# A chunked delta-rule attention with two dense layers: the first block solve done as two 16-row triangles joined by products, and the weights loaded from ScalarE's queue

## The chip, the cores and the metric

The kernel runs on one core of one Trainium2 chip. The metric is the device time of one execution in microseconds (us); the times below are those of three executions and of one profiled execution. The engines are TensorE (PE, matrix products), VectorE (DVE), ScalarE (ACT), GpSimd (POOL) and SyncE (SP, which only issues transfers).

## What is computed

A linear attention with a delta rule for each of 4 x 8 heads over 768 steps, with a state of 48 x 48 for each head; its output (3072 tokens of 384) runs through two dense layers.

```python
k_n = k / (np.linalg.norm(k, axis=-1, keepdims=True) + 1e-06)
for t in range(S):
    kt, vt, bt = (k_n[:, :, t], v[:, :, t], beta[:, :, t, None])
    y[:, :, t] = np.einsum('bhd,bhde->bhe', q[:, :, t], state)
    v_old = np.einsum('bhde,bhd->bhe', state, kt)
    state = state + bt[:, :, :, None] * np.einsum('bhd,bhe->bhde', kt, vt - v_old)
...
h = x @ w_in                       # 384 -> 1024
solu = h * softmax(h)
ln = (solu - mu) / np.sqrt(var + 1e-06) * g_ln
x = ln @ w_out                     # 1024 -> 384
...
h = x @ w_in                       # 384 -> 2048
g = h * (1.0 / (1.0 + np.exp(-1.702 * h)))
y = g @ w_out                      # 2048 -> 384
```

## The kernel before, in words

The 768 steps are cut into 24 chunks of 32 (`CH`), numbered n; four chunks are a macro step m. Within a chunk the rule is solved for all steps at once: with the products of the chunk's normalised k vectors in a lower triangle, the inverse of that triangle, applied to v minus what the state already holds, gives the chunk's updates. The parts are functions, and each of them adds tasks to a planner.

- `weights` (lines 443 to 506), called 42 times by `all_weights`: one slice of a weight matrix. The matrices come as 8-byte floats. SP issues the load of the raw words (L462, the only place where weights are loaded), ACT takes the high word's magnitude (L465), DVE merges the low word's bits and the sign in three steps (L467, L469, L477), ACT makes the fp16 high part (L490), PE forms the rest by products with an identity (L496, L497) and ACT stores it as the fp16 low part (L499), or DVE does it alone (L502). Staging buffers are few (`stg`, and pieces of other tensors lent to it while those are unused), so a load's issue waits until the slice before in its buffer is done. Every dense product later is three fp16 products of high and low parts.
- `gram(n)` (lines 545 to 581): PE forms k by k and k by q for the chunk (L554), DVE masks them (L569), SP stores both to DRAM (L579, L581), which turns them round for the solve.
- `solve(m)` (lines 584 to 660), one system of 32 x 32 for each of 128 rows (4 chunks x 8 heads x 4 batches) side by side on DVE: the load of the triangles `tri` (L588), norms by three steps of an iteration (L596 to L610), a scaling of `tri` (L615), ones on the diagonal (L618) and the elimination. Step j multiplies column j of the rows below j by row j (L624) and adds it to those rows (L627). For m = 0 this is one task, `whole`, with each step cut in two pieces; for m > 0 the 60 instructions are 60 tasks among DVE's other work. Then the inverse is scaled into `dsb` (L643), stored (L653) and loaded back by chunk as `dt` (L658).
- `recur(n)` (lines 661 to 798), the chain through the state: v is scaled on POOL (L714); for n > 0 PE applies the state to k (L726) and DVE subtracts (L730), giving `r_`; PE multiplies `r_` by the chunk's inverse (`dr_`, L735, 32 small fp32 products); ACT copies the result beside the state (L742; from a certain n on DVE does half of them, L746); PE forms the chunk's output (L752) and the state's update (L787, or L782), which DVE adds (L796).
- `layer1(n)` (lines 801 to 887): DVE takes the output's scale (L816), it is split into fp16 parts and transposed, PE multiplies by `w1` (L834), then softmax and normalisation on DVE, ACT and POOL (L841 to L881), and a transpose into `lnt` (L887). `layer1_out(g)` works on a group of 2 or 4 chunks: products with `wo1` (L906), written as `x2th` by ACT (L910) and `x2tl` by DVE (L913). `layer2(g)`: `w2` (L941), the gate (L946 to L958), `wo2` (L968), and the store of the result.

`busy` (L344, L345) lets PE multiply zeros wherever the planner sees it idle in the early part; below these are the filler products.

The order is a planner's (`Plan`): it is a list scheduler with a cost for every task, run while the program is built. A task's priority is the due time of its chunk (`due`) plus constants from `PRM` and an offset from the table `OFF`. It writes one fixed stream per engine, and on the chip each engine runs its stream strictly in order, waiting at semaphores. So everything in an engine's stream behind a waiting instruction waits too. A DMA task's issue stands in the stream of the engine that issues it. The order in which the functions are called, in the loop at the end of the kernel, gives the dependencies: before the change, `gram(4..7)` and `solve(1)` are called ahead of `recur(0)`.

```python
for n in range(first[g], first[g] + cnt):
    if n % SUB == 0 and n // SUB + 1 < NMAC:
        for n2 in range(n + SUB, n + 2 * SUB):
            gram(n2)
        solve(n // SUB + 1)
    layer1(n, recur(n))
layer1_out(g)
layer2(g)
```

## Time and profile before

| | us |
|---|---|
| median of 3 executions | 838.25 |
| lowest, highest | 837.28, 838.33 |
| profiled execution, time | 838.51 |
| profiled execution, span of the profile | 836.8 |

The profiled execution's time is 1.7 us more than its span: that lies outside the instructions that the profile records. All times of the trace count from the span's start. A line L462 is line 462 of the kernel before. "A<-B" beside a time means that the engine waited for A's producer B.

### The profile page before, as it was taken

What the parts mean: (1) busy time and instruction counts of PE and PEld (TensorE: products, weight loads), DVE (VectorE), ACT (ScalarE), POOL (GpSimd) and SP (SyncE); (2) the same over time, 40 slices, a digit from 0 to 9 for tenths busy, and PEclk for the clock granted to TensorE, in tenths of its full rate; (3) what the DMA queues carried; (4) which work ended last, traced back from release to release, by engine and by line L of the source; (5) the groups of instructions that cost most, each with busy time, mean ns of one, the idle gap of its engine ahead of it and who ended that gap; (6) DMA issues with size and microseconds to landing.
All of it is one profiled execution on the core that took longest, in us unless ns stands there. A gap on an engine that the chain in (4) does not pass through costs nothing.

```text
span 836.8 us, 25071 instructions
## 1 busy us (share of the span) xinstructions
PE 765.9 (92%) x10461; PEld 415.1 (50%) x10461; DVE 595.7 (71%) x1557; ACT 375.8 (45%) x695; POOL 252.0 (30%) x249
## 2 busy tenths in 40 slices
PE   6538889999899999998999999999999999999997
PEld 3224555677666744444444444444545444444443
DVE  1896978999998978999889889996655456311111
ACT  1425734466555513455543455345553436422332
POOL 3002010232214433434531445324442314330322
PEclk7658999999999999999999999999999999999999
DMA  7797878966666465638874365346543333011001
GB/s 177 226 254 178 225 158 192 241 105 173 151 123 168 99 137 149 156 90 187 161 203 125 91 167 107 102 127 153 136 64 92 114 60 47 16 26 38 1 0 38
DMA packets 177745, 105.75 MB, mean 126 GB/s; under 512 B 128320, under 2 KB 161984, under 8 KB 177632
## 3 DMA queue, kind: packets, MB, share of 16 engines
q1 hardware_dynamic: 177632, 104.15, 53.0%
q8 instruction: 82, 1.34, 0.7%
q14 instruction: 31, 0.25, 0.1%
HBM read 66.16 MB, written 20.64 MB: 104 GB/s over the span
## 4 chain that ended last, share of the span: by engine, by line
PE 35%; DVE 14%; issue 3%; ACT 2%; DMA 1%; SPq 1%; POOL 0%; POOLq 0%; ACTq 0%; DVEq 0%
PE psum L941 11%; PE psum L968 11%; PE psum L906 5%; PE psum L834 4%; DVE trt L624 2%; DVE tri L627 2%; DVE th L949 1%; DVE mv L746 1%; DVE mv L796 1%; PE psum L735 1%; PE psum L752 1%; ACT mv L742 1%; DMA stg<-udr 1%; PE psum L726 1%; DVE eb L853 1%
## 5 line engine op out<-in xcount | busy, mean ns | idle before, releaser
L955 POOL TENSOR_TENSOR gl<-th,gh 128x512 f16<-128x512 f32 (+1 forms) x105 | 114.2, 1089 | 226.4 <-ACT gh L952 154.3
L949 DVE SCALAR_TENSOR_TENSOR th<-th,psum 128x512 f32<-128x512 f32 (+1 forms) x112 | 67.8, 607 | 85.8 <-ACT th L946 85.2
L968 PE MATMUL psum<-gh,wo2h 128*128 128x512 f16 (+1 forms) x336 | 117.8, 350 | 1.6 <-ACT ob L979 1.2
L968 PE MATMUL psum<-gl,wo2h 128*128 128x512 f16 (+1 forms) x336 | 117.5, 350 | 1.7 <-POOL gl L955 1.4
L968 PE MATMUL psum<-gh,wo2l 128*128 128x512 f16 (+1 forms) x336 | 117.4, 350 | 1.1 <-ACT wo2l L499 1.1
L941 PE MATMUL psum<-x2th,w2h 128*128 128x512 f16 (+1 forms) x336 | 117.8, 351 | 0.3 <-DVE ysb L823 0.2
L941 PE MATMUL psum<-x2th,w2l 128*128 128x512 f16 (+1 forms) x336 | 117.6, 350 | 0.0
L941 PE MATMUL psum<-x2tl,w2h 128*128 128x512 f16 (+1 forms) x336 | 117.6, 350 | 0.0
L946 ACT ACTIVATE th<-psum 128x512 f32<-128x512 f32 (+1 forms) x112 | 59.3, 531 | 97.4 <-PE psum L941 96.9
L952 ACT ACTIVATE gh<-th 128x512 f16<-128x512 f32 (+1 forms) x112 | 63.2, 566 | 74.5 <-DVE th L949 72.7
L968 PEld LDWEIGHTS <-wo2h 128*128 128x128 f16 x672 | 65.8, 98 | 62.3 <-issue 4.5
L834 PE MATMUL psum<-w1h,xt 128*128 128x512 f16 x288 | 93.6, 384 | 2.3 <-DMA xt<-ysb 1.4
L941 PEld LDWEIGHTS <-w2h 128*128 128x128 f16 x672 | 64.2, 98 | 57.2 <-issue 0.6
L624 DVE TENSOR_TENSOR trt<-tri 128x58 f32<-128x58 f32 (+29 forms) x209 | 80.3, 395 | 2.8
L627 DVE TENSOR_TENSOR tri<-tri,trt 128x58 f32<-128x58 f32 (+29 forms) x209 | 79.0, 390 | 2.3
L834 PEld LDWEIGHTS <-xt 128*128 128x128 f16 x432 | 41.3, 99 | 51.0 <-issue 3.9
L850 ACT ACTIVATE eb<-psum,col 128x512 f32<-128x512 f32 x48 | 36.9, 772 | 61.2 <-DVE col L846 53.2
L796 DVE SCALAR_TENSOR_TENSOR mv<-psum,mv 48x384 f32<-48x384 f32 x92 | 51.0, 555 | 16.5 <-PE psum L782 14.1
L883 POOL TENSOR_TENSOR lnr<-eb,lnr 128x1024 f16<-128x1024 f32 x24 | 51.3, 2139 | 35.7 <-ACT lnr L881 35.7
L906 PE MATMUL psum<-lntl,wo1h 128*128 128x512 f16 (+1 forms) x168 | 58.6, 349 | 0.9 <-DMA lntl<-lnr 0.9
L906 PE MATMUL psum<-lnth,wo1h 128*128 128x512 f16 (+1 forms) x168 | 58.6, 349 | 0.0
L906 PE MATMUL psum<-lnth,wo1l 128*128 128x512 f16 (+1 forms) x168 | 58.6, 349 | 0.0
(191 smaller groups left out, 1228.3 us busy)
## 6 DMA issues: line engine op xcount, KB each, us to landing
kq<-kq SPq DMA_DIRECT2D x44, 192.0 KB, 4.6
stg<-w_in SPq DMA_DIRECT2D x11, 512.0 KB, 5.9
vt<-vt SPq DMA_DIRECT2D x24, 192.0 KB, 3.5
st<-qt SPq DMA_DIRECT2D x48, 96.0 KB, 2.4
stg<-udr SPq DMA_DIRECT2D x48, 96.0 KB, 2.4
kt<-kdr SPq DMA_DIRECT2D x48, 96.0 KB, 2.8
ktr<-kd SPq DMA_DIRECT2D x46, 96.0 KB, 3.5
stg<-w_out SPq DMA_DIRECT2D x11, 384.0 KB, 5.5
```

The lines of the kernel that those rows point to most:

```text
L624: DVE.tensor_tensor(out=tv, in0=tri[:, lo:hi, j:j + 1].to_broadcast([128, nr, j]), in1=tri[:, j:j + 1, 0:j].to_broadcast([128, nr, j]), op ...
L627: DVE.tensor_tensor(out=tri[:, lo:hi, 0:j], in0=tri[:, lo:hi, 0:j], in1=tv, op=ALU.add)
L796: P.add("DVE", dve(384), lambda sv=sv, r0=r0, e=e: DVE.scalar_tensor_tensor(out=sv, in0=bank(b4[e])[r0:r0 + D, 0:H * D], scalar=1.0 / (KS_ ...
L834: PE.matmul(bank(bh[j]), lhsT=x[:, k], rhs=w_[:, k, 512 * j:512 * j + 512], start=(k == 0 and i == 0), stop=(k == K0 - 1 and i == 2))
L883: P.add("POOL", pool(F1), lambda: POOL.tensor_tensor(out=lnr[1], in0=e_, in1=lnr[0], op=ALU.subtract), r=["lnrh"] + [f"eb{ie}_{j}" for j i ...
L906: PE.matmul(bank(ba)[:, 0:w_], lhsT=wo1[a][:, k, oc], rhs=lnt[b][:, k, tk], start=(k == 0 and i == 0), stop=(k == K1 - 1 and i == 2))
L941: PE.matmul(bank(bh)[:, 0:w_], lhsT=w2[a][:, k, fc], rhs=x2t[b][:, k, tk], start=(k == 0 and j == 0), stop=(k == K0 - 1 and j == 2))
L946: P.add("ACT", act(w_), lambda: ACT.activation(out=th, in_=bank(bh)[:, 0:w_], func=ACTF.Tanh, scale=0.851 / (X2S * W2S)), r=[bh], w=[f"th{ ...
L949: P.add("DVE", dve(w_), lambda: DVE.scalar_tensor_tensor(out=th, in0=th, scalar=1.0, in1=bank(bh)[:, 0:w_], op0=ALU.add, op1=ALU.mult), r= ...
L952: P.add("ACT", act(w_), lambda: ACT.activation(out=gh, in_=th, func=ACTF.Copy), r=[f"th{i}"], w=[f"gh{i}"], prio=base)
L955: P.add("POOL", pool(w_), lambda: POOL.tensor_tensor(out=gl, in0=th, in1=gh, op=ALU.subtract), r=[f"th{i}", f"gh{i}"], w=[f"gl{i}"], prio= ...
L968: PE.matmul(bank(acc[o])[:, 0:w_], lhsT=wo2[a][:, f, oc], rhs=gb[i][b][:, 0:w_], start=(f == 0 and j == 0), stop=(f == K2 - 1 and j == 2))
```

## The change

The first system (m = 0) is no longer eliminated whole. `halves` sets the lower left 16 x 16 block to zero and eliminates the two 16 x 16 triangles on the diagonal at once, by a view `blocks` of the tensor that has the two triangles as a second axis. The inverse that it leaves is block diagonal. What is missing, the effect of the first 16 steps of a chunk on the last 16, is put into the recurrences of chunks 0 to 3: `first_` applies the block-diagonal inverse to `r_`, ACT copies the result, `over_` multiplies it by the lower left block of the k products (`below`, which `gram` now keeps for these chunks, masked by `cross`), DVE subtracts that from `r_`, and then `dr_` runs as before. Weight loads are issued by ACT instead of SP, somewhat earlier in priority, and the planner keeps a DMA clock for each of the two issuers. `gram(4..7)` and `solve(1)` are called behind `recur(3)`. One tile of zeros serves both uses. All numbers in `OFF` and `PRM` are new.

```diff
+    trip = T("trip", [128, CH * CH + CH])
+    tri = trip[:, 0:CH * CH].rearrange("p (i j) -> p i j", j=CH)
+    blocks = trip.rearrange("p (a x) -> p a x", a=2)[:, :, 0:512].rearrange("p a (i c) -> p a i c", c=CH)
+    cross = T("cross", [128, CH])
...
+        def corner():
+            POOL.memset(cross, 1.0)
+            POOL.memset(cross[:, 0:CH // 2], 0.0)
+            for b in range(B):
+                x = cross[32 * b:32 * b + 32, CH // 2:]
+                POOL.affine_select(out=x, in_=x, pattern=[[0, CH // 2]], base=CH // 2,
+                                   channel_multiplier=-1, compare_op=ALU.is_gt, fill=0.0)
...
-            P.add("SP", ISSUE, lambda: SP.dma_start(out=raw.rearrange("p n t -> p (n t)"), in_=src.bitcast(I32)),
-                  w=key, prio=prio, lat=dma(n * 1024), nb=PRM["nb"] if nst[0] <= PRM["nk"] else PRM["nb2"])
+            P.add("ACT", ISSUE, lambda: ACT.dma_start(out=raw.rearrange("p n t -> p (n t)"), in_=src.bitcast(I32)),
+                  w=key, prio=prio - PRM["wl"], lat=dma(n * 1024), nb=PRM["nb"] if nst[0] <= PRM["nk"] else PRM["nb2"])
...
         if m == 0:
+            P.add("DVE", dve(256), lambda: DVE.tensor_tensor(
+                out=below[s], in0=bank(bk).rearrange("p (h c) -> p h c", h=H)[:, :, 0:CH],
+                in1=cross.unsqueeze(1).to_broadcast([128, H, CH]), op=ALU.mult),
+                r=[bk, "cross"], w=[belowk[s], f"below{s}"], prio=base + PRM["bl"])
...
-            def whole():
-                for j in range(1, CH - 1):
-                    mid = j + 1 + max(1, round((CH - 1 - j) * PRM["cut"]))
-                    cuts = [(j + 1, mid), (mid, CH)] if mid < CH else [(j + 1, CH)]
-                    for part in range(2):
-                        for c in cuts:
-                            eliminate(j, part, *c)
-            P.add("DVE", 23.2, whole, w=["tri"], prio=base, port=True)
+            def halves():
+                DVE.memset(tri[:, CH // 2:, 0:CH // 2], 0.0)
+                for j in range(1, CH // 2 - 1):
+                    nr = CH // 2 - 1 - j
+                    tv = trt[:, 0:2 * nr * j].rearrange("p (a i c) -> p a i c", a=2, c=j)
+                    rows = blocks[:, :, j + 1:CH // 2]
+                    DVE.tensor_tensor(out=tv, in0=rows[:, :, :, j:j + 1].to_broadcast([128, 2, nr, j]),
+                                      in1=blocks[:, :, j:j + 1, 0:j].to_broadcast([128, 2, nr, j]), op=ALU.mult)
+                    DVE.tensor_tensor(out=rows[:, :, :, 0:j], in0=rows[:, :, :, 0:j], in1=tv, op=ALU.add)
+            P.add("DVE", 6.4, halves, w=["tri"], prio=base, port=True)
...
+        if m == 0:
+            bo, bw = Bank(SIDE), Bank(SIDE)
...
+                PE.matmul(hd(bo)[q, h, :], lhsT=dt[q, s, h, 0:CH], rhs=r_[q, h, :], start=True, stop=True,
...
+                PE.matmul(hd(bw)[q, h, :], lhsT=below[s][q, h, :], rhs=v_[q, h, :], start=True, stop=True,
...
+            quads(first_, 0.78, [f"dt{md}_{s}", f"r{ir}"], [bo], base, 0.21)
+            P.add("ACT", act(384), lambda: ACT.activation(out=v_, in_=hd(bo), func=ACTF.Copy),
+                  r=[bo], w=[f"vt{iv}"], prio=base)
+            quads(over_, 0.78, [f"vt{iv}", belowk[s], f"below{s}"], [bw], base, 0.21)
+            P.add("DVE", dve(384), lambda: DVE.tensor_tensor(out=r_, in0=r_, in1=hd(bw), op=ALU.subtract),
+                  r=[bw], w=[f"r{ir}"], prio=base)
         quads(dr_, 0.78, [f"dt{md}_{s}", f"r{ir}"], [b2] + mvw, base, 0.21)
...
-            if n % SUB == 0 and n // SUB + 1 < NMAC:
+            if n and n % SUB == 0 and n // SUB + 1 < NMAC:
...
-            layer1(n, recur(n))
+            y = recur(n)
+            if n == SUB - 1:
+                for n2 in range(SUB, 2 * SUB):
+                    gram(n2)
+                solve(1)
+            layer1(n, y)
```

In the changed kernel the lines have moved: the weight load L462 is L477, the weight steps L465, L467, L469, L477 are L480, L482, L484, L492, and L496, L497 are L511, L512; the triangle's load L588 is L607, its scaling L615 is L634, `dr_` L735 is L758, ACT's copy L742 is L783, the output's product L752 is L793, the state update L782 is L823 and L787 is L828, and the filler L345 is L352. New are L590 (`below`), L650 to L657 (`halves`), L766 and L771 (`first_`, `over_`), L774 (ACT's copy) and L777 (DVE's subtraction).

On DVE, at the first solve, the rows before, from the scaling of the triangles to the elimination's first step (`tri` is the triangles, `trt` a scratch tensor, `nrm` the norms):

```order
L615 TENSOR_TENSOR tri_126<-tri_126,nrm_133 128x1024
L618 MEMSET tri_126 128x32
L624 TENSOR_TENSOR trt_127<-tri_126 128x14
L624 TENSOR_TENSOR trt_127<-tri_126 128x16
L627 TENSOR_TENSOR tri_126<-tri_126,trt_127 128x14
```

and now (`trip` holds the triangles, `fst`, `lnth` a weight slice on its way):

```order
L634 TENSOR_TENSOR trip_126<-trip_126,nrm_134 128x1024
L484 SCALAR_TENSOR_TENSOR fst2_89<-fst2_89,lnth_90 128x512
L637 MEMSET trip_126 128x32
L482 TENSOR_SCALAR lnth_90<-lnth_90 128x512
L650 MEMSET trip_126 128x16x16
L655 TENSOR_TENSOR trt_128<-trip_126 128x28
L657 TENSOR_TENSOR trip_126<-trip_126,trt_128 128x2x14
L655 TENSOR_TENSOR trt_128<-trip_126 128x52
L657 TENSOR_TENSOR trip_126<-trip_126,trt_128 128x2x13x2
```

The 30 steps of four or two instructions have become 14 of two, and steps of weight slices stand among the rows ahead of them.

On SP, near the start, the rows before, where the stores of the k products (`gdr`), the weight loads (from `w_in`) and the triangle's load share one stream:

```order
L579 DMA gdr0_140<-gsb1_123 128x8x32
L579 DMA gdr0_140<-th0_100 128x8x32
L462 DMA stg2_86<-w_in 128x1024
L579 DMA gdr0_140<-gsb0_122 128x8x32
L462 DMA stg0_84<-w_in 128x1024
L462 DMA stg1_85<-w_in 128x1024
L579 DMA gdr0_140<-th1_101 128x8x32
L408 DMA bt_132<-bt 128x192
L462 DMA lntl_91<-w_in 128x1024
L462 DMA lnth_90<-w_in 128x1024
L588 DMA tri_126<-gdr0_140 128x1024
```

and now the head of ACT's stream, where the weight loads have gone:

```order
L477 DMA stg2_86<-w_in 128x1024
L477 DMA stg0_84<-w_in 128x1024
L477 DMA stg1_85<-w_in 128x1024
L480 ACT_TABLE_LOAD
L480 ACTIVATE fst2_89<-stg2_86 128x512
L477 DMA wo2h_82<-w_out 128x768
L480 ACTIVATE fst0_87<-stg0_84 128x512
L477 DMA wo2h_82<-w_out 128x768
L477 DMA wo2l_83<-w_out 128x768
L480 ACTIVATE fst1_88<-stg1_85 128x512
```

SP has no weight load left, and three of them are ACT's first instructions; the later ones stand among ACT's computing.

On PE, at the recurrence of chunk 0, the rows before, with a filler ahead and a weight slice's product behind:

```order
L345 MATMUL psum0_63<-zeros1_157 128x512
L735 MATMUL psum5_68<-rb0_131,dt0_129 32x48 x32
L496 MATMUL psum4_67<-w2h_80,eye_72 128x384
L497 LDWEIGHTS neg_73
L497 MATMUL psum4_67<-wo1h_78,neg_73 128x384
...
L752 MATMUL psum5_68<-mv_117,st0_115 32x48 x32
```

and now, where four fillers stand between `first_` and `over_`, and a weight slice's products between `over_` and `dr_`:

```order
L766 MATMUL psum5_68<-rb0_132,dt0_130 32x48 x32
L352 LDWEIGHTS zeros0_157
L352 MATMUL psum0_63<-zeros0_157 128x512
...
L771 MATMUL psum7_70<-vt0_120,gh0_103 32x48 x32
L511 MATMUL psum4_67<-w2l_81,eye_72 128x384
L512 LDWEIGHTS neg_73
L512 MATMUL psum4_67<-wo1h_78,neg_73 128x384
L758 MATMUL psum6_69<-rb0_132,dt0_130 32x48 x32
```

The one group of products ahead of the state has become three in a row, each of which needs the one before.

## Rows read from the trace of the kernel before

**Rows 1.** The page: busy us, share of the span and instructions of each engine

```profile
PE 765.9 (92%) x10461; PEld 415.1 (50%) x10461; DVE 595.7 (71%) x1557; ACT 375.8 (45%) x695; POOL 252.0 (30%) x249
```

**Rows 2.** Windows: length, busy PE, PEld, DVE, ACT, POOL, PE clock, DMA share, GB/s

```profile
0.00:76.80 76.80, 41.79 (x710) 20.92 (x710) 52.27 (x195) 23.32 (x41) 10.09 (x26) 0.67 0.85 220
0.00:31.30 31.30, 19.49 (x541) 11.16 (x542) 10.65 (x22) 7.49 (x12) 6.56 (x24) 0.73 0.74 184
39.00:60.40 21.40, 6.06 (x131) 3.76 (x129) 20.64 (x120) 5.21 (x9) 0.00 (x0) 0.50 0.97 263
76.80:156.50 79.70, 71.94 (x1641) 42.29 (x1641) 65.35 (x182) 43.77 (x87) 7.06 (x6) 0.96 0.79 183
200.00:550.00 350.00, 329.99 (x5065) 185.83 (x5063) 315.77 (x798) 165.01 (x312) 133.97 (x127) 0.99 0.60 140
550.00:826.00 276.00, 274.81 (x2518) 129.88 (x2517) 119.54 (x270) 113.11 (x194) 84.81 (x74) 1.00 0.28 63
```

**Rows 3.** Windows of line 345, the fillers, alone: PE, PEld, clock, DMA, GB/s

```profile
0.00:76.80 76.80, 15.57 (x43) 5.17 (x43) 0.67 0.85 220
76.80:156.50 79.70, 14.85 (x55) 5.08 (x54) 0.96 0.79 183
```

**Rows 4.** DVE's timeline, both ends of the elimination: start, duration, engine, line, operation

```profile
39.03 0.14 DVE L624 TENSOR_TENSOR trt<-tri 128x14 f32<-128x14 f32 x1
39.06 0.09 DVE L618 MEMSET tri<- 128x32 f32 x1
...
59.92 0.19 DVE L624 TENSOR_TENSOR trt<-tri 128x30 f32<-128x30 f32 x1
60.15 0.19 DVE L627 TENSOR_TENSOR tri<-tri,trt 128x30 f32<-128x30 f32 x1
```

**Rows 5.** PE's timeline, the first `dr_` and the first product with `wo1`

```profile
76.84 0.88 PE L735 MATMUL psum<-rb,dt 32*32 32x48 f32 x64
...
156.54 0.27 PE L906 MATMUL psum<-lnth,wo1h 128*128 128x256 f16 x1
```

**Rows 6.** DVE's timeline, three steps of the second solve

```profile
187.07 0.28 DVE L627 TENSOR_TENSOR tri<-tri,trt 128x130 f32<-128x130 f32 x1
...
189.06 0.23 DVE L624 TENSOR_TENSOR trt<-tri 128x84 f32<-128x84 f32 x1
...
191.21 0.18 DVE L624 TENSOR_TENSOR trt<-tri 128x30 f32<-128x30 f32 x1
```

**Rows 7.** ACT's timeline, the copies behind the first `dr_` (in brackets: idle before, releaser)

```profile
77.85 1.96 ACT L742 ACTIVATE mv<-psum 32x384 f32<-32x384 f32 x4 [0.57 <-PE psum L735]
```

**Rows 8.** SP's timeline, issues of transfers near the start

```profile
9.90 0.82 SPq L462 DMA_DIRECT2D stg<-w_in  x1
...
19.16 0.38 SPq L579 DMA_DIRECT2D gdr<-th  x1
...
23.22 0.33 SPq L462 DMA_DIRECT2D lntl<-w_in  x1
23.60 1.21 SPq L462 DMA_DIRECT2D lnth<-w_in  x1
24.91 0.37 SPq L588 DMA_DIRECT2D tri<-gdr  x1
```

**Rows 9.** DVE's timeline, the first mask and the first subtraction

```profile
7.08 0.42 DVE L569 TENSOR_TENSOR gsb<-psum,mask 128x256 f32<-128x256 f32 x1 [6.08 <-PE psum L554]
...
88.09 0.54 DVE L730 TENSOR_TENSOR rb<-vt,psum 128x384 f32<-128x384 f32 x1
```

**Rows 10.** Line 462's waits and issues: count, ns min/median/max, first and last start in us

```profile
L462 SPq EVENT_SEMAPHORE  x27: 17/28/4503, 20.2 to 220.8; - x27
L462 SPq DMA_DIRECT2D stg<-w_in x11: 333/377/1345, 9.9 to 200.9; - x11
```

**Rows 11.** DVE's timeline, two steps of a weight slice

```profile
29.88 0.69 DVE L477 SCALAR_TENSOR_TENSOR lntl<-lntl 128x512 int32<-128x512 int32 x1
30.48 0.42 DVE L467 TENSOR_SCALAR lnth<-lnth 128x512 int32<-128x512 int32 x1
```

More of the change, by code (lines that the diff above doesn't have):

```diff
@@ L148, in emit @@
         pend = {}
-        dma_free = 0.0
+        dma_free = {"SP": 0.0, "ACT": 0.0}
         bank_free = [0.0] * 8
@@ L176, in emit @@
                     if t.lat:
[L177 removed]
+                        st = max(st, dma_free[e] - PRM["la"])
                     ok = True
@@ L232, in emit @@
             if t.lat:
-                s2 = max(dma_free, st + dur)
-                dma_free = s2 + t.lat
-                t.end = s2 + t.lat + LAND
+                s2 = max(dma_free[t.eng], st + dur)
+                both = min(dma_free["ACT" if t.eng == "SP" else "SP"] - s2, t.lat)
+                dma_free[t.eng] = s2 + t.lat + max(0.0, 0.7 * both)
+                t.end = dma_free[t.eng] + LAND
             else:
```

20 lines of the change are left out of this document (14 added, 6 removed).

## The prediction

> **What bounds the kernel now.** I read the page's busy shares first. TensorE (PE) is busy 92% of the span [rows 1], which looks like a kernel that only less PE work could shorten. The windows by stage say otherwise for the first part. From 550 to 826 us PE is full (274.81 of 276 us). Between 200 and 550 it works 329.99 of 350 us while VectorE (DVE) works 315.77: PE is the bound there, with 20.0 us of idle time. Until 76.8 us PE shows 41.79 us and DVE 52.27 of 76.8, and from 76.8 to 156.5 PE shows 71.94 and DVE 65.35 of 79.7 [rows 2]. PE's share ahead of 156.5 is padded: 15.57 us and 14.85 us of it are the filler products on zeros [rows 3], which nobody waits for. Without them PE has 26.2 us of work until 76.8 and 57.1 us from there to 156.5, less than DVE in both. So the front of the kernel, up to the first product of layer 1's second matrix at 156.54 us, is set by a chain and by DVE's order; from there on PE has 680 us of its own work, and whatever brings the 156.54 forward brings the end forward.
>
> That front is one chain. The first 32x32 systems are eliminated on DVE from 39.03 to 60.15 + 0.19 = 60.34 [rows 4]; the first recurrence's product `dr_` starts at 76.84 and the first product with `wo1` at 156.54 [rows 5]. During the elimination DVE is busy 20.64 of 21.4 us, and PE 6.06 at a granted clock of 0.50 [rows 2]: nobody else makes progress there.
>
> **The change, part by part.** Line numbers of the changed kernel are written "new L".
>
> *Elimination.* It goes from 118 instructions in 21.3 us to a memset and 28 instructions over 28 to 112 elements in each of 128 rows. The second system's steps, which are not split, give the price: 0.18 us for 30 wide, 0.23 for 84, 0.28 for 130 [rows 6]. Twenty-eight between 28 and 112 wide at about 0.235 us are 6.6 us, and 28 gaps of 0.04 (from 59.92 + 0.19 to 60.15 [rows 4]) 1.1 us. The memset of a 16x16 block in each row isn't in this trace: 0.09 us is the memset of 32 elements [rows 4], 0.42 the mask over 256 [rows 9]; I take 0.25, since its size is the latter's and its work the former's. Sum 7.9: **-13.4 us** on the solve's path.
>
> *Coupling.* For chunks 0 to 3 the triangles are joined by `first_` (32 products), a copy on ScalarE (ACT), `over_` (32 products) and a subtraction on DVE, all ahead of `dr_`. The old `dr_`, 64 rows for its 32 float32 products, took 0.88 us [rows 5], and each new group has its form, so 0.88. The copy is at least the 0.48 of 32 rows (four in 1.96 us, with 0.57 from the end of the product to the first) [rows 7]; the subtraction has the form of L730, 0.54 [rows 9]. With 0.1 us for each hand-over: 0.88 + 0.13 + 0.5 + 0.1 + 0.88 + 0.13 + 0.55 + 0.1 = **+3.3 us** per chunk on the chain. That is once ahead of `dr_` of chunk 0; for chunks 1 to 3 it lies beside layer 1's work as long as that fills DVE (if not: a rival). Bounds per chunk: 2.8 (no hand-over seen) and 5.1 (0.57 at each of four). PE also gets 8 groups x 0.82 = 6.6 us, in place of filler, and DVE 4 masks (new L590) at 0.42. The six instructions on GpSimd that make `cross` precede everything and wait for nothing.
>
> *Weight loads.* On SyncE (SP) the first weight load is issued at 9.90, between the stores of the products' results, and the load of the triangle (L588) leaves at 24.91, right behind 0.33 + 1.21 us of weight issues that began at 23.22 [rows 8]. Now ACT issues three weight loads as its first instructions, SP has none, and the load of the triangle can go as soon as the last store (19.16) has landed: about 22.5, **-2.5 us** (ends: -4.5, from the widest wait at a weight issue, 4.50 [rows 10], and +8.2, below).
>
> The Trainium skill speaks against this part: "DMA: Bandwidth & Descriptors", section "Issuing engines are not separate DMA queues", says that DMAs of several issuers run on the same 16 engines, interleave, and save only issue time. By that rule the term would be the 1.5 us of issues at best; by the row it is 2.5, and since the next paragraph shows that DVE ends later than this path, the sum would be the same by either. What the rule can take away is a rival.
>
> In the trace the engines are 74% busy at 184 GB/s in the first 31.3 us [rows 2]: the free quarter, 8.1 us, is about what three loads of 0.5 MB need (1.5 MB / 184 GB/s = 8.2 us). If they take it from the k loads instead, the solve starts 8.2 us later; I take nothing, since the share is free.
>
> *When `dr_` of chunk 0 starts.* By the solve's path: 76.84 - 13.4 - 2.5 + 3.3 = 64.2. But DVE runs its stream in order, and the new order puts more ahead: before the first subtraction it has 19 rows of each of the three weight steps where 12, 14 and 14 stood, 9 masks more, and the coupling. Seven L467 at 0.42 and ten L469/L477 at 0.69 [rows 11] are 9.8, some only 384 wide, so 9.0; the masks are 9 x 0.42 = 3.8; so DVE has 52.3 - 13.4 + 9.0 + 3.8 + 0.5 = 52.2 us to do. It starts with the first mask at 7.08 [rows 9]. Before, it idled 76.8 - 7.1 - 52.3 = 17.4 us of that, 13.6 of them ahead of 31.3. With weights in SBUF earlier I leave it 8: 7.1 + 52.2 + 8 = **67.3**, 9.5 us earlier than 76.84 (idle of 5 gives 64.3, where the solve's path ends too; of 13 gives 72.3).
>
> *From there to the first `wo1` product.* DVE is at 82% here; what the order adds between the first L816 (the first chunk's result) and the first L913 (the first group's result of `wo1`) is three couplings (1.4), 1.3 weight slices (2.3), six steps of the second solve, whose place moves behind recurrence 3 (2.2); it loses two masks (0.7) and the third chunk's share of layer 1, which isn't needed for the first group (4.0). Net +1.3: the first `wo1` product comes 9.5 - 1.3 = **8.2 us earlier**, near 148. The issues that ACT takes over ahead of it (14 x 0.38 us, the median of their old issue being 0.377 [rows 10]) are 5.3 us against 79.7 - 43.77 = 36 us in which ACT is free [rows 2].
>
> *Behind it.* PE's work is the same. DVE has about 12.4 us less there: eight weight slices (10.7) and four masks that now lie in front. PE idles 20.0 us between 200 and 550 [rows 2]; how much of that DVE causes the windows don't tell, so the bounds are 0 and -12. I take **-2**, near the lower end, because DVE's 90% is no full engine. The tables that set the order move much else there, which I cost at nothing: PE's 94% hides what comes a few us sooner or later.
>
> Sum: -8.2 - 2 = -10.2 on the profiled execution's 838.5, which stands 0.26 above the median of the runs (838.25): **828.0 us**.
>
> **The rivals.** *More gain.* DVE's early idle goes down to 5 us (-12.5 + 1.3 = -11.2) and DVE's lighter load removes half of PE's 20 us of idle time: 838.3 - 21.2 = about 817 (812 to 823). For it: the loads are issued at once. Against: between 200 and 550 the state chain, too, sets PE's waits.
>
> *Nothing left, by the coupling.* Layer 1 doesn't cover the couplings of chunks 1 to 3: 3 x 3.3 = 9.9 us come back before the first `wo1` product, -10.2 + 9.9, about 838. Against it: DVE's 65.35 of 79.7 us leave 14.4 us, and the four recurrences wait for layer 1's rows in DVE's order as much as for one another.
>
> *Nothing left, by the transfers.* The early weights share the engines with the k loads, as the rule above has it: the solve's path ends at 64.2 + 2.5 + 8.2 = 74.9, 1.9 us earlier than before, of which 1.3 go again: about 837.7. For it: the engines are at 74% in the mean, and could be full where it matters.
>
> *Slower: ACT's queue is held.* ACT works in order. A load's issue waits until its staging buffer is free; on SP that wait reached 4.50 us [rows 10], and cost nothing behind it but loads. Now the copies of `first_` and of `dr_` (new L774, L783), which each recurrence's chain needs, stand behind such an issue: in the new order up to five stand between two of these copies. At 4.5 us in each of the four early recurrences, 18 us are lost: 838.3 - 10.2 + 18 = 846 (840 to 848). It decides the sign from 10.2 / 4 = 2.6 us for each recurrence. Against it: the median wait there is 0.028 us [rows 10], and the tile that an issue overwrites is read by steps placed well ahead.
>
> *The change doesn't do what it says* if the triangles' 28 instructions run at a longer duration than rows 6 give; at 0.4 with its gap each it would be 11.5 us, 3.6 more, and since DVE's load is then 3.6 longer the total is near 832: inside the forecast's range.
>
> **How the numbers follow.** My forecast (824 to 832, from idle of 5 to 12 and 0 to -4 behind) has 0.58; more gain 0.14; nothing left, both ways, 0.13; slower 0.15. A measurement of this kernel can tell 0.2%, 1.7 us, from no change: same is 836.6 to 839.9. The cases of nothing left split about evenly between just faster (0.06) and the same (0.07). So faster 0.78, same 0.07, slower 0.15. The range runs from 814, which leaves out the tail of more gain, to 840, which leaves out nearly all of the slower case: some 0.82 of the chance is inside. The forecast's own range is 824 to 832.
>
> **What would show it.** In the profile of the changed kernel: an elimination of 7 to 9 us with 28 instructions; the triangle's load near 22.5; the chunk-0 `dr_` between 64 and 72 and not before its subtraction; the first `wo1` product near 148; PE still the full engine behind it, with 16 to 20 us of idle time between 190 and 540. I am wrong if `dr_` is early but `wo1` isn't (the couplings, or ACT's copies behind weight issues, seen as idle time of DVE and PE released by ACT), or if the triangle's load lands later than before.

## The result and the profile after

The changed kernel takes **848.88 us** (median of 4 executions, 845.84 to 849.92), the kernel before 837.76 in the same comparison (4 executions, 834.68 to 838.33). The ratio is 1.0123, 95% interval 1.0081 to 1.0165: slower by 11 us, where 828.0 and a gain of 10 were forecast. The profiled execution took 847.86 us, its span 845.8.

The page's line of busy times, against [rows 1]:

```profile
PE 778.7 (92%) x10964; PEld 425.0 (50%) x10964; DVE 585.7 (69%) x1476; ACT 378.5 (45%) x699; POOL 248.2 (29%) x255
```

DVE has 10 us less to do, PE 13 more: 7.3 of them are the couplings' products (L766 3.53, L771 3.73), and at the lower of its clocks the same products take longer (below, 1.50 instead of 0.88 us). The windows of [rows 2] (busy PE, PEld, DVE, ACT, POOL, PE clock, DMA share, GB/s), and those of the fillers alone [rows 3]:

```profile
0.00:76.80 76.80, 49.22 (x920) 25.73 (x921) 48.59 (x132) 34.66 (x66) 9.96 (x32) 0.76 0.96 248
0.00:31.30 31.30, 18.72 (x523) 10.32 (x527) 12.04 (x29) 8.71 (x14) 7.60 (x30) 0.78 0.99 247
39.00:60.40 21.40, 11.35 (x138) 5.78 (x138) 18.60 (x63) 8.29 (x16) 0.00 (x0) 0.52 0.98 257
76.80:156.50 79.70, 70.27 (x1665) 42.35 (x1664) 59.00 (x170) 39.41 (x76) 6.33 (x6) 0.85 0.80 201
200.00:550.00 350.00, 329.98 (x5067) 190.76 (x5065) 318.13 (x788) 165.05 (x312) 136.09 (x131) 0.99 0.59 135
550.00:826.00 276.00, 273.63 (x2565) 129.52 (x2564) 119.76 (x278) 117.27 (x200) 86.92 (x77) 1.00 0.29 67
```

```profile
0.00:76.80 76.80, 11.99 (x38) 3.94 (x38) 0.76 0.96 248
76.80:156.50 79.70, 14.39 (x43) 4.77 (x44) 0.85 0.80 201
```

The late windows stand as they were. In the first 31.3 us the DMA share has gone from 0.74 to 0.99. DVE's timeline, the wait for the triangles and both ends of the elimination:

```profile
40.47 0.19 DVE L615 TENSOR_SCALAR nrm<-trip 128x32 f32<-128x32 f32 x1 [4.63 <-DMA trip<-gdr]
...
48.68 0.27 DVE L650 MEMSET trip<- 128x256 f32 x1
48.87 0.12 DVE L655 TENSOR_TENSOR trt<-trip 128x28 f32<-128x28 f32 x1
...
56.34 0.19 DVE L657 TENSOR_TENSOR trip<-trip,trt 128x28 f32<-128x28 f32 x1
```

The elimination takes 56.53 - 48.68 = 7.85 us. It begins 9.6 us later than before [rows 4]. SP's timeline shows why (the last load of k, the store of the last products, then the triangles' load):

```profile
10.65 0.31 SPq L562 DMA_DIRECT2D lntl<-kq  x1
...
25.60 0.39 SPq L598 DMA_DIRECT2D gdr<-th  x1
...
30.93 2.59 SPq L699 DMA_DIRECT2D kt<-kt  x2
33.62 1.21 SPq L607 DMA_DIRECT2D trip<-gdr  x1
```

The last load of k was issued at 4.04 before, now at 10.65. The last store went at 19.16, the triangles' load at 24.91 [rows 8]; now at 25.60 and 33.62, right behind two other issues of 2.59 us. PE's timeline: `first_` (L766), `over_` (L771) and `dr_` (L758) of chunks 0 and 1, and the first product with `wo1`:

```profile
71.49 0.88 PE L766 MATMUL psum<-rb,dt 32*32 32x48 f32 x64
...
75.25 0.88 PE L758 MATMUL psum<-rb,dt 32*32 32x48 f32 x64
...
93.86 0.88 PE L766 MATMUL psum<-rb,dt 32*32 32x48 f32 x64
...
103.10 0.54 PE L771 MATMUL psum<-vt,gl 32*32 32x48 f32 x32 [0.28 <-DVE psb L584]
104.36 0.54 PE L771 MATMUL psum<-vt,gl 32*32 32x48 f32 x32 [0.72 <-issue]
...
108.87 0.88 PE L758 MATMUL psum<-rb,dt 32*32 32x48 f32 x64
...
167.23 0.28 PE L947 MATMUL psum<-lnth,wo1h 128*128 128x256 f16 x1
```

Chunk 0's `dr_` is 1.6 us earlier than before, chunk 1's 20 us later (88.73 before), and the first `wo1` product comes at 167.23 instead of 156.54 [rows 5]. From there to the end of the span it is 678.6 us, 680.3 before. So the loss lies wholly ahead of that product, and the experiments ask what sets its time.

### The profile page after: what moved, and what is told of

Read it like the earlier page. It is cut to its first block, busy times and chain, and to the rows that moved or that the text cites. A ratio compares the mean times of both kernels' runs of the same rounds, so it can differ in the third digit from the quotient of the medians.

```text
span 845.8 us, 25981 instructions
## 1 busy us (share of the span) xinstructions
PE 778.7 (92%) x10964; PEld 425.0 (50%) x10964; DVE 585.7 (69%) x1476; ACT 378.5 (45%) x699; POOL 248.2 (29%) x255
## 5 line engine op out<-in xcount | busy, mean ns | idle before, releaser
L996 POOL TENSOR_TENSOR gl<-th,gh 128x512 f16<-128x512 f32 (+1 forms) x105 | 110.4, 1052 | 279.4 <-ACT gh L993 197.2
L646 DVE TENSOR_TENSOR trip<-trip,trt 128x30 f32<-128x30 f32 (+9 forms) x150 | 67.4, 449 | 2.8
L643 DVE TENSOR_TENSOR trt<-trip 128x30 f32<-128x30 f32 (+9 forms) x150 | 66.6, 444 | 2.7
L924 POOL TENSOR_TENSOR lnr<-eb,lnr 128x1024 f16<-128x1024 f32 x24 | 53.2, 2217 | 29.3 <-ACT lnr L922 29.3
L837 DVE SCALAR_TENSOR_TENSOR mv<-psum,mv 48x384 f32<-48x384 f32 x92 | 51.1, 555 | 12.1 <-PE psum L823 7.3
```

The lines of the kernel that those rows point to most:

```text
L643: DVE.tensor_tensor(out=tv, in0=tri[:, lo:hi, j:j + 1].to_broadcast([128, nr, j]), in1=tri[:, j:j + 1, 0:j].to_broadcast([128, nr, j]), op ...
L646: DVE.tensor_tensor(out=tri[:, lo:hi, 0:j], in0=tri[:, lo:hi, 0:j], in1=tv, op=ALU.add)
L837: P.add("DVE", dve(384), lambda sv=sv, r0=r0, e=e: DVE.scalar_tensor_tensor(out=sv, in0=bank(b4[e])[r0:r0 + D, 0:H * D], scalar=1.0 / (KS_ ...
L924: P.add("POOL", pool(F1), lambda: POOL.tensor_tensor(out=lnr[1], in0=e_, in1=lnr[0], op=ALU.subtract), r=["lnrh"] + [f"eb{ie}_{j}" for j i ...
L996: P.add("POOL", pool(w_), lambda: POOL.tensor_tensor(out=gl, in0=th, in1=gh, op=ALU.subtract), r=[f"th{i}", f"gh{i}"], w=[f"gl{i}"], prio= ...
```

## The experiments

Eighteen kernels were run, numbered in the order in which they were thought of; the ratio is to the kernel before on the same chip. "Same order" means that the instructions stand in the planned order of the kernel named, with only the edit put in.

| run | what it is | time, us | ratio and interval | first `dr_` | first `wo1` | span |
|---|---|---|---|---|---|---|
| | before | 837.76 | 1 | 76.84 | 156.54 | 836.8 |
| | after | 848.88 | 1.0123 [1.0081, 1.0165] | 75.25 | 167.23 | 845.8 |
| e13 | before, halves only | 837.87 | 1.0024 [0.9999, 1.0048] | 76.62 | 154.54 | 833.1 |
| e14 | before, couplings only | 851.56 | 1.0197 [1.0166, 1.0227] | 78.57 | 169.49 | 850.7 |
| e15 | before, both | 850.18 | 1.0176 [1.0144, 1.0208] | 78.86 | 166.66 | 846.7 |
| e4 | before, loads from ACT | 845.25 | 1.0086 [1.0054, 1.0118] | 82.49 | 161.35 | 844.0 |
| e5 | before, 1.5 MB more | 838.50 | 1.0032 [1.0006, 1.0058] | 78.19 | 156.11 | 835.5 |
| e16 | before, half-size loads | 838.26 | 1.0007 [0.9976, 1.0038] | 80.84 | 155.68 | 836.7 |
| e17 | e13, half-size loads | 825.20 | 0.9847 [0.9786, 0.9907] | 72.36 | 146.54 | 823.6 |
| e18 | after, half-size loads | 835.94 | 0.9961 [0.9926, 0.9997] | 70.56 | 155.85 | 833.5 |
| e1 | after, first loads later | 850.76 | 1.0155 [1.0094, 1.0215] | 78.01 | 171.45 | 848.1 |
| e2 | after, no couplings | 844.32 | 1.0095 [1.0063, 1.0126] | 77.80 | 164.58 | 843.7 |
| e3 | after, late loads on SP | 847.24 | 1.0143 [1.0083, 1.0203] | 76.33 | 163.12 | 844.6 |
| e9 | after, more fillers | 848.23 | 1.0149 [1.0083, 1.0216] | 77.15 | 169.12 | 845.9 |
| e12 | after, `wo1` earlier | 857.28 | 1.0225 [1.0194, 1.0256] | 74.75 | 162.82 | 849.1 |

The last three columns are those of one profiled execution of each kernel; its time can lie some us from the median in the row (6 below it in e12, 3 in e13), so differences between kernels are taken from the ratios. Span less first `wo1` is 676.7 to 682.6 us in all of these but e12 (686.3).

### The two additions, one at a time, in the order of before

e13 puts the halved elimination into the kernel before and leaves the couplings out (so the lower left block of the inverse is missing from its result); e14 puts only the couplings in, with a block of zeros as the lower left one, all of it ahead of `dr_` in one piece; e15 does both (again without that block).

```diff
-                for j in range(1, CH - 1):
-                    mid = j + 1 + max(1, round((CH - 1 - j) * PRM["cut"]))
...
+                DVE.memset(tri[:, CH // 2:, 0:CH // 2], 0.0)
+                for j in range(1, CH // 2 - 1):
...
+            def coupled(plain=last.fn):
...
+                for i, a, x in ((1, dt[:, s, :, 0:CH], r_), (2, None, v_)):
...
+                        ACT.activation(out=v_, in_=far(1), func=ACTF.Copy)
+                    else:
+                        DVE.tensor_tensor(out=r_, in0=r_, in1=far(2), op=ALU.subtract)
+                plain()
```

> The kernel before with its fixed order and its weight loads on SP; only the elimination of the first systems is replaced by the one of two halves, with no couplings, so the lower left block of chunks 0 to 3 is left out of the result. Theory K (as forecast: what the elimination gains reaches the end): the first dr_ at 63 to 66 instead of 76.8, the first wo1 product 10 us or more earlier, 824 to 829. Theory J (other waits of the front take the gain): the first dr_ as early as that, the first wo1 product at 152 or later, 832 to 837.

> The kernel before with its fixed order, weights on SP and whole elimination; ahead of dr_ of chunks 0 to 3 the chain of the couplings is added (32 products, ACT's copy, 32 products, DVE's subtraction) with a block of zeros, so that it changes nothing in the result. Theory K (layer 1 covers the couplings of chunks 1 to 3): 838 to 842. Theory J (four couplings lie on the chain that sets the front, or hold PE, ACT and DVE in their fixed orders): 844 to 852.

> e13_before_halves and e14_before_couple together: the first part of the change alone, weights on SP, in the fixed order of the kernel before (the block of zeros instead of the lower left block, which is left out of the result). Theory K: 828 to 832, as the sum of the forecast without the weights' part. Theory J: 838 to 846.

**Halves only: nothing.** In e13 the elimination ends 12.5 us earlier, and `dr_` starts 0.22 us earlier; both theories on record had it at 63 to 66. DVE's timeline of e13, from the elimination's last step to the first output:

```profile
47.64 0.19 DVE L640 TENSOR_TENSOR trip<-trip,trt 128x28 f32<-128x28 f32 x1
...
62.13 0.55 DVE L479 SCALAR_TENSOR_TENSOR w2l<-wo2l,w2l 128x384 int32<-128x384 int32 x1
80.75 0.56 DVE L820 TENSOR_REDUCE col<-psum 128x1 f32<-128x384 f32 x1 [18.07 <-PE psum L756]
```

and the same wait in the kernel before:

```profile
73.57 0.56 DVE L477 SCALAR_TENSOR_TENSOR w2l<-wo2l,w2l 128x384 int32<-128x384 int32 x1
80.97 0.56 DVE L816 TENSOR_REDUCE col<-psum 128x1 f32<-128x384 f32 x1 [6.84 <-PE psum L752]
```

What the elimination gave up, DVE waits: 18.07 instead of 6.84 us. The windows of e13 (columns as above) and ACT's waits from 39 to 77 us (us in total, times, longest) show who is busy then:

```profile
39.00:60.40 21.40, 7.88 (x134) 4.55 (x135) 19.40 (x56) 5.60 (x10) 0.00 (x0) 0.50 0.98 271
60.00:70.00 10.00, 6.05 (x16) 2.16 (x15) 2.67 (x7) 3.41 (x8) 0.00 (x0) 0.67 0.97 283
```

```profile
ACT w2h L467 <- DMA wo2h<-w_out: 4.3, 2, 2.4
ACT w2l L501 <- PE psum L499: 3.8, 2, 3.2
ACT w2l L467 <- DMA stg<-w_out: 3.0, 1, 3.0
ACT fst L467 <- DMA lnth<-w_in: 3.0, 1, 3.0
```

No engine is near full from 60 to 70 us, but the DMA engines are, at 283 GB/s. ACT waits for slice after slice of the weights. PE's stream has products of four of those slices, with fillers between, ahead of `dr_`. What `dr_` itself needs was there 5 us before it: POOL's scaling of v, which waits for the inverse, ends at 71.53. POOL's row, and PE's from the wait for a slice to `dr_`:

```profile
70.69 0.84 POOL L718 TENSOR_TENSOR rb<-vt,dt 128x384 f32<-128x384 f32 x1 [62.97 <-DMA dt<-ddr]
```

```profile
68.71 0.59 PE L499 MATMUL psum<-w2h,neg 128*128 128x512 f16 x1 [3.95 <-ACT w2h L492]
...
76.62 0.88 PE L739 MATMUL psum<-rb,dt 32*32 32x48 f32 x64
```

SP's stream, too, has loads for k and weights ahead of the inverse's store, which left at 61.59 though the inverse was ready at 51.1. Two of these k loads wait for PE's k products, 4.7 us together.

**Couplings only: 14 to 16 us more.** PE's timeline of e14, `first_` (L749) and `dr_` (L735) of each chunk:

```profile
75.39 0.88 PE L749 MATMUL psum<-rb,dt 32*32 32x48 f32 x64
...
78.57 0.90 PE L735 MATMUL psum<-rb,dt 32*32 32x48 f32 x64 [0.75 <-DVE rb L754]
...
90.36 0.88 PE L749 MATMUL psum<-rb,dt 32*32 32x48 f32 x64
...
95.90 1.50 PE L735 MATMUL psum<-rb,dt 32*32 32x48 f32 x64 [0.65 <-DVE rb L754]
...
119.40 1.50 PE L749 MATMUL psum<-rb,dt 32*32 32x48 f32 x64
...
123.74 1.50 PE L735 MATMUL psum<-rb,dt 32*32 32x48 f32 x64 [0.68 <-DVE rb L754]
...
142.83 0.88 PE L749 MATMUL psum<-rb,dt 32*32 32x48 f32 x64
...
145.93 1.39 PE L735 MATMUL psum<-rb,dt 32*32 32x48 f32 x64 [0.68 <-DVE rb L754]
```

From `first_` to `dr_` it is 3.18 + 5.54 + 4.34 + 3.10 = 16.2 us. The median rises by 16.3, the profiled span by 13.9, and the first `wo1` product comes 13.0 later. `dr_` of the four chunks comes 1.7, 7.2, 10.2 and 14.1 us later than before (76.84, 88.73, 113.59, 131.82): each coupling adds to the delay of the one before, and little covers them. In the second, 2.26 us are a pause of PE (below); in the third the products run at the lower clock (1.50 instead of 0.88 us). With both edits (e15) the loss is 14.9. That is 1.4 less than in e14, but the two intervals overlap, so the 12.5 us of the elimination give back nothing that can be told. So the halved solve with its couplings is by itself 1.8% slower in the order of before, without ACT's loads and without a new order.

### Is it the transfers?

Three kernels load only the first half of the words of every weight slice (the rest of each buffer is zeroed once, so the weights' other halves are missing from the result): e16 is the kernel before, e17 is e13, e18 the changed kernel, each in its own order.

```diff
-  lambda: SP.dma_start(out=raw.rearrange("p n t -> p (n t)"), in_=src.bitcast(I32))
+  lambda: SP.dma_start(out=raw.rearrange("p n t -> p (n t)")[:, 0:n], in_=src.bitcast(I32)[:, 0:n])
```

> The kernel before, same order, but every weight load brings only the first half of its words (half the bytes; the rest of the buffer is zeroed once by 11 memsets on DVE ahead of everything, so the weights are left wrong). Theory K (the stretch until the first recurrence is bound by transfers as well as by the elimination): the elimination still ends near 60 here, so the first dr_ comes only a little earlier, 73 to 77, and DVE's wait for the first output stays near 6 us; time 832 to 838. Rival L (the order alone holds the front; transfers don't matter): dr_ 76 to 78, time as before. This run is the base for the next one.

> The kernel before with the halved elimination, without couplings (as in the earlier run, lower-left block left out), and with half-size weight loads. Theory K: what took the 12 us of the shorter elimination in the earlier run was the weights' arrival (DMA share 0.97 to 1.0 from 39 to 70 us, ACT waiting for every slice); with half the bytes the first dr_ comes at 64 to 71 instead of 76.6, the wait of DVE for the first output shrinks from 18 to 7 to 13 us, and, if the rest follows, the first wo1 product comes 4 to 10 us before 154.5 and the time is 4 to 9 us below that of the half-size loads alone. Rival L: dr_ again at 75 to 78 (something in the order other than transfers holds it), time equal to the half-size loads alone. Theory M (dr_ comes early, but the chain behind it or the planner's order loses it): dr_ at 64 to 71, wo1 and time unchanged within 2 us.

> The changed kernel, same order, with half-size weight loads. Theory K: the triangles' load is issued at 26 to 30 instead of 33.6, first_ comes 5 to 9 us earlier than 71.5, dr_ at 67 to 71; the couplings of chunks 1 to 3 stay, so the time is 838 to 845, 4 to 9 below 848.9. Rival L: triangles earlier, but first_ at 70 to 72 and the time 846 to 850. Theory M: dr_ early, second dr_ still near 109 and time 846 to 850.

The zeroing costs more than was thought: it sets the triangles' load back to 31.6 us in e16 and 32.2 in e17 (24.91 before). In e16 that delays the chain; in e17, whose solve is shorter, it does not. SP's store of the inverse in e13, e16 and e17, one row each:

```profile
61.59 0.83 SPq L657 DMA_DIRECT2D ddr<-dsb  x2
...
69.69 0.79 SPq L656 DMA_DIRECT2D ddr<-dsb  x2
...
61.39 1.14 SPq L660 DMA_DIRECT2D ddr<-dsb  x2
```

In the kernel before it left at 63.73. In e16, moreover, POOL's scaling of v takes 5.62 us, from 75.17 to 80.79 (2.73 in the kernel before, 0.84 in e13 and e17). `dr_` follows it at 80.84, 4.0 us later than in the kernel before, where 73 to 77 were expected. So e16 is as fast as the kernel before although its solve is late, and what fewer bytes alone are worth there is not shown.

The pair that differs in the bytes, with a delay only on the side of fewer bytes, is e13 and e17: `dr_` comes 4.3 us earlier, `wo1` 8.0, and the ratio goes from 1.0024 to 0.9847, about **15 us**. So with the shorter elimination the bytes of the weights set the time. DVE's wait in e17, its `dr_` and its first `wo1` product, from DVE's and PE's timelines:

```profile
76.49 0.56 DVE L823 TENSOR_REDUCE col<-psum 128x1 f32<-128x384 f32 x1 [8.91 <-PE psum L759]
```

```profile
66.89 0.38 PE L502 MATMUL psum<-w2h,neg 128*128 128x512 f16 x1 [2.71 <-ACT w2h L495]
...
72.36 0.88 PE L742 MATMUL psum<-rb,dt 32*32 32x48 f32 x64
...
146.54 0.27 PE L913 MATMUL psum<-lnth,wo1h 128*128 128x256 f16 x1
```

The inverse's store leaves no earlier than in e13. The slice on which PE waits comes 1.8 us earlier (66.89 instead of 68.71); most of the rest of the 4.3 is PE at a higher clock behind it (seven fillers take 1.67 us instead of 3.19). `dr_` fell just short of the interval that was expected (64 to 71).

Against e16, e17 is 838.26 - 825.20 = 13 us faster, with `dr_` 8.5 and `wo1` 9.1 us earlier. But 6.0 us of the solve's lead are the zeroing's (69.69 less 63.73), so the shorter elimination with half the bytes is worth 7 to 13 us, an estimate from these rows; with all of them it was worth nothing.

The changed kernel gains too: from 848.88 to 835.94, 13 us, or 1.0123 to 0.9961 by the ratios, more than was expected. Its triangles' load leaves only 1.5 us earlier (32.17), with the zeroing ahead of it; its first two `dr_` come 4.7 and 5.8 us earlier. So the bytes of the weights cost time in both kernels with the shorter elimination. What stays in e18 against e17, 10.7 us, is the couplings with the new order and ACT's issues; no run separates these three there.

e5 put three more loads of 0.5 MB, into DRAM that nobody reads, at the head of ACT's stream in the kernel before; e4 issues all weight loads of the kernel before from ACT, each at the place in the order where SP issued it.

```diff
+            P.add("POOL", 0.0, lambda spare=spare, src=src: ACT.dma_start(out=spare, in_=src.bitcast(I32)), prio=-3000, port=False)
...
-            P.add("SP", ISSUE, lambda: SP.dma_start(out=raw.rearrange("p n t -> p (n t)"), in_=src.bitcast(I32)),
+            P.add("SP", ISSUE, lambda: ACT.dma_start(out=raw.rearrange("p n t -> p (n t)"), in_=src.bitcast(I32)),
```

> The kernel before, its order unchanged, with three loads of 0.5 MB more, issued by ACT as its first instructions into memory that nobody reads. Theory A (early weight loads take the transfer engines from the k loads): the triangles' load is issued 6 to 9 us later than 24.9 and the time is 843 to 847. Theory B (the transfer engines have room; the triangles are late in the changed kernel through its order): within 2 us of 24.9, 835 to 839.

> The kernel before with its fixed order, all weight loads issued by ACT instead of SP at the same places of the common order. Theory A: the loads start about when they did, 836 to 841. Theory C: ACT's queue is held as in the changed kernel, 844 or more.

In e5 SP's last load of k, which waits for no semaphore, is issued at 9.80 instead of 4.04:

```profile
9.80 0.31 SPq L551 DMA_DIRECT2D lntl<-kq  x1
```

So ACT's loads hold not only the transfers but SP's issues as well. The triangles' load goes 3.45 us later (28.36; 6 to 9 or under 2 were expected), `dr_` 1.35 later and `wo1` not later at all; the time is 0.3% longer. So by the first `wo1` product the kernel before has absorbed the delay. In e4 the load goes on time (24.94), but ACT, whose stream is in order, is held. Its timeline:

```profile
24.99 0.34 ACTq L462 DMA_DIRECT2D lntl<-w_in  x1
25.37 0.67 ACT L465 ACTIVATE fst<-stg 128x512 f32<-128x512 f32 x1 [18.38 <-PE psum L554]
```

The issue behind which ACT waits writes `lntl`, which the k products still read. The elimination then starts at 44.09 instead of 39.03, and the time rises by 0.86%. In the changed kernel the planner knows that ACT issues, and no such wait is left there: ACT's 19 semaphore instructions at L477 take 0.017 us in the median, 2.06 at most.

### Rivals inside the changed kernel

e3 moves the weight loads from the 19th on back to SP; e9 adds 36 fillers between the k products, for the clock; e1 lets the first three loads wait until the third k load has landed; e2 leaves the couplings' instructions out (so the lower left block is missing from its result).

```diff
-            P.add("ACT", ISSUE, lambda: ACT.dma_start(
+            P.add("ACT", ISSUE, lambda e=(ACT if nst[0] <= 18 else SP): e.dma_start(
...
+                if last[0].startswith("gram") and 50.0 < st < 125.0:
+                    for _ in range(4):
+                        self.fill[0][2]()
```

> The changed kernel with its fixed order, but the weight loads from the 19th on are issued by SP instead of ACT, at the same places of the common order. Theory A: same within 2 us, 846 to 850. Theory C (issues hold ACT's queue and with it the copies of the recurrences): 6 us or more come back, 842 or less.

> The changed kernel with its fixed order and 36 filler products more, four behind each group of k products that the order places between the first and the last of the early recurrences (7.8 us of PE at 2.4 GHz). Theory F (PE's pauses of 1.7 to 3 us inside a group, each followed by a stretch at 1.2 GHz, come from many small products in a row, whose code is loaded in pieces): the pauses between the first dr_ and the first wo1 product fall from 10 us to 5 or less, that stretch from 92 to 84 to 88 us, the time to 841 to 845. Theory G (the stretch is long because the couplings stand late in the engines' orders): the fillers only cost, 848 to 853.

> The changed kernel with its fixed order, but ACT first reads one element of the third chunk's k load and only then issues its first three weight loads. Theory A (the early weight loads take the transfer engines from the k loads, and the couplings stretch the early recurrences): the load of the triangles is issued at 25 to 28 us instead of 33.6, the first product of the first recurrence starts 5 to 8 us earlier, the time is 840 to 844. Theory B (the triangles are late through SP's order and PE's pauses, not through the transfers): the load stays at 32 to 34 us and the time at 847 to 850.

> The changed kernel with its fixed order, without the couplings: the products first_ and over_, ACT's copy and DVE's subtraction are left out for chunks 0 to 3, so the lower left block of these chunks' systems is left out of the result. Theory A: about 4 us come back ahead of the first recurrence's product and 6 to 10 behind it, 834 to 838. Theory C (behind the first recurrence the loss is weight issues that hold ACT's queue, or PE at 1.2 GHz after pauses, not the couplings): only the 4 us come back, 843 to 846.

e3 gains nothing that its interval can tell, where 6 us or more were expected if issues in ACT's queue hold the recurrences. e9 raises the clock between 75 and 170 us from 0.86 to 0.93 and leaves the time as it was. Its fillers also keep PE busy 3 us longer there (87.01 instead of 83.89), so the run doesn't tell whether the lost clock was filled with waiting or the fillers took what it gave back.

In e1 SP's last load of k is issued at 4.05 again, the triangles' load goes 2.9 us earlier and the norms 3.4. But DVE's stream has slices of the late weights ahead of the masks (the second mask runs at 15.08, at 12.97 in the changed kernel) and ahead of the elimination, which starts at 49.25, later than the 48.68 of the changed kernel. So e1 trades one delay for another, and the load met neither theory's interval.

e2 gives back 4.6 us by the medians and 2.3 by the ratios, whose intervals overlap; the couplings' 16 us of e14 aren't there. Its `dr_` of chunk 1 stays at 112.70. Between the first two `dr_` PE is busy 29.79 of 34.90 us in e2, 29.58 of 33.62 in the changed kernel and 11.55 of 11.89 in the kernel before: the order made for the couplings puts some 18 us more of PE's other work there, and it stays when they go. In the changed kernel the second coupling spans 93.86 to 108.87: `over_` stands behind 18 products of `w1` and a group of k products. What the new order costs or gives by itself was not tried.

### Another order

e12 sets two thirds of the first group's `wo1` products ahead of the fourth recurrence's output.

```diff
+        up = [x for x in seq if x[0] is not None and x[0].hoist == 1]
+        at = [x[0] is not None and x[0].hoist == 0 for x in seq].index(True)
+        seq = [x for x in seq[:at] if x not in up] + up + [x for x in seq[at:] if x not in up]
```

> The changed kernel with its fixed order, but for PE around the first wo1 product: two thirds of the first group's wo1 products (5.3 us) stand ahead of the fourth recurrence's output and state update instead of behind them, in two banks of PSUM that are free then. Theory H (the first wo1 product waits for nothing of its own but stands behind the fourth recurrence in PE's fixed order): it starts 4 to 6 us earlier, near 162, and the time is 842 to 846. Theory I (what is moved up there is lost again, since the fourth recurrence's delay reaches the second group): the first wo1 product is earlier, the time is 847 to 851.

`wo1` starts 4.4 us earlier, and the time is 8 us longer: what was moved up is lost behind it, and more. That the rest waits for the recurrence that was pushed back is likely, not shown. A first `wo1` product is a good mark of progress only as long as what lies ahead of it stays the same.

Two more tries moved the rest of recurrences 1 to 3 right behind ACT's copy, alone (e10) and with e3's and e9's edits (e11): 854.87 us, 1.0229 [1.0161, 1.0297], and 847.74, 1.0159 [1.0098, 1.0219]. Three let the planner make the order anew: with weights on SP and the new tables (e6: 854.85, 1.0214 [1.0164, 1.0263]), with weights on SP and the tables of before (e7: 860.07, 1.0280 [1.0223, 1.0337]), and with the whole elimination, no couplings and weights on ACT (e8: 868.37, 1.0376 [1.0338, 1.0415]). These orders cost 6 to 20 us more than the changed kernel's, perhaps because their tables were made for another program, so the times say nothing about the parts. One thing they do show: with all bytes loaded, e6 and e7 have their first `dr_` at 69.95 and 68.43, couplings included, though the first `wo1` product of e6 comes only at 175.5. So it is not the transfers alone that hold `dr_` in e13, but the transfers in an order that puts their slices ahead of it.

## Why the prediction was wrong

**Right.** The elimination: 7.9 forecast, 7.85 measured. The price of one coupling: 3.3 forecast, 3.2 and 3.1 in e14 where nothing disturbs it. "Whatever brings the 156.54 forward brings the end forward": `wo1` to the end is 678.6 after 680.3, and within 676.7 to 682.6 in every run of the table but e12; the -2 behind it was about right too (-1.7). The rival of ACT's held queue was rightly given little, as far as e3 can tell; that the time came out just above its 840 to 848 is chance.

**Where the sum went wrong,** in the profiled executions: the first `dr_` came 1.6 us earlier (9.5 forecast), and from there to the first `wo1` product it took 12.3 us more (91.98 after 79.70), where the sum had 1.3 more (its parts add to 1.2). Three steps led there.

**Wrong, first step: "the front of the kernel ... is set by a chain and by DVE's order."** The sum took the front's length from DVE's load (52.2 us, with idle of 8 left to it) and put DVE's 13.4 us on the path. The changed kernel's DVE has only 48.59 us in the first 76.8, and idles the other 28. "Nobody else makes progress there" was said of the elimination with [rows 2] at hand, whose window from 39.00 to 60.40 gives the DMA engines a share of 0.97 at 263 GB/s. The transfers made progress there: the elimination hid them. Without that cover the same slices arrive at the same time, and `dr_`, which stands behind them on PE and, through the inverse's store, on SP, starts at the same time (e13). e17 shows the other half: with fewer bytes e13 is some 15 us faster.

**Wrong, second step: the transfers at nothing, "since the share is free".** The term was -4.5 to +8.2, with -2.5 taken for the triangles' load. The load went 8.7 us later (33.62 instead of 24.91) and the norms 9.2 (40.47 instead of 31.30): beyond the upper end. 0.74 was a mean over 31.3 us, and the three loads, issued at once, met the k loads in the stretch where the solve's path needs them. e5 puts what these three do alone at 3.45 us, and e1 gets 2.9 back. The other 5 us or so are not separated: more weights are loaded early (247 GB/s instead of 184 over 31.3 us, 7.7 MB instead of 5.8), steps of weight slices stand between DVE's masks, and SP's order has two issues of 2.59 us right ahead of the load. This was the rival "by the transfers"; it had the direction, and put it at 9.6 us against the forecast. The rule of the Trainium skill that was weighed there ("DMA: Bandwidth & Descriptors", section "Issuing engines are not separate DMA queues") is what the trace shows: loads from ACT and SP share the engines, whose share went to 0.99.

**Wrong, third step: couplings of chunks 1 to 3 "beside layer 1's work".** That DVE was at 82% there says that DVE has room, not that the recurrences have. They are a chain, and in the order of before e14 shows all four couplings on it, 14 to 16 us. The rival "by the coupling" had it, at 9.9 us, too small by the pause and the lower clock. The fillers that the couplings were to replace stayed for the most part: 26.4 us of them after, 30.4 before. In the changed kernel the couplings' own share is small (e2), and chunk 1's `dr_` is 20 us late by PE's order. That "the tables that set the order move much else" was put at nothing, and only for the part behind `wo1`; ahead of it there was no term for it.

**The fault that joins them.** The two rivals were treated as alternatives, each of which takes back the gain. In the order of before both came true (e13, e14), and together they make a loss (e15); no case of the prediction had that. Their sum, -10.2 + 9.6 + 9.9 on 838.3, is 847.6, and 847.86 was measured, but that is luck: without couplings it would be 837.7, and e2 takes 844.32. How the 11 us of the changed kernel divide among transfers, couplings and the new order stays open.

## What to carry to other kernels

When a long stretch of one engine is shortened, look at what runs beside it, the DMA engines' share above all: at 0.97 the stretch is hiding transfers, and if the order puts what they bring ahead of the chain, they become the bound. Test that by loading fewer bytes in both kernels, not only by looking at who waits, and check that the edit which saves the bytes doesn't delay the chain itself, as the zeroing did here. A part taken out of a fixed order doesn't show what it costs: the order around it stays. And ask of rivals whether they exclude one another: two that take back the gain on different resources make a loss together.

## What the runs showed of the hardware

PE pauses in or behind a group of small products without waiting for anything that the profile shows. Four such pauses lie in the changed kernel between 76.8 and 167 us, where the kernel before has one. The first, in PE's timeline, and the DMA queues from 78.6 to 79.2 us (packets, MB, share):

```profile
77.07 1.20 PE L569 MATMUL psum<-kq 48*32 48x64 f32 x69
81.30 0.97 PE L569 MATMUL psum<-kq 48*32 48x64 f32 x28 [3.03 <-issue]
```

```profile
q8 instruction: 1, 0.02, 10.2%
```

In each of the four (81.30, 116.66, 147.07 and 161.85; 3.03, 2.17, 2.57 and 1.68 us) one packet of about 16 KB of the queue "instruction" starts 2.4 to 2.5 us ahead of the pause's end (at 78.82, 114.27, 144.54 and 159.46). 14 such packets lie between 77 and 157 us, so most of them are not felt. The groups concerned are long runs of small products, of which the couplings add eight. The Trainium skill ("Runtime: NRT & Kernel Launch", section "Instruction fetch mechanics") has instructions refilled in blocks of 16 KiB, hidden behind the issue of those before; if the pauses are these refills, as the packets suggest, they are not hidden in these four places. Loads in flight are not what the four have in common: the DMA engines' share during them is 0.87, 0.19, 0.25 and 0.79. No run was made to move such a packet.

The granted clock between 76.8 and 156.5 us fell from 0.96 to 0.85, to the lower of the two levels (0.50, 1.2 GHz) from 80 to 90 us and from 120 to 125. Both stretches begin in or behind such a pause. What it cost here no run shows: e9 raised it, with fillers, and the time stayed.

POOL's scaling of v for chunk 0 is the same instruction in these kernels. It took 0.84 us in e13 and e17, where DVE is idle beside it, 1.31 in the changed kernel (DVE busy 1.30 of it), 2.73 in the kernel before (2.03) and 5.62 in e16 (4.92). So it can take far longer beside a busy DVE, though not by a fixed share, and in e16 `dr_` waited for it.
